# Gathers held to their turns, scatters moved behind a branch, and one set of codes a turn later, in an attention and mixture-of-experts kernel

## The chip, the cores and the metric

The kernel runs on one core of a Trainium2 chip. The metric is the device time of one execution in microseconds (us); the time given for the kernel before is the median of three runs. PE is the matrix engine (TensorE), PEld its weight loads, DVE is VectorE, ACT is ScalarE, POOL is GpSimd, and SP is the engine that here only issues loads and stores.

## The reference

Two blocks stand one behind the other. The first is attention among clusters: query and key attend to each other only where both have the same nearest centroid. The second is a mixture of experts with one expert per token, chosen by cosine similarity.

```python
# B, H, S, D = 4, 8, 768, 64; 16 clusters for each head
q_assign = argmax(einsum('bhsd,hcd->bhsc', q_n, c_n), -1)   # q_n, c_n: normalized
k_assign = argmax(einsum('bhsd,hcd->bhsc', k_n, c_n), -1)
scores = q @ k.T / sqrt(D), with -1e9 where q_assign != k_assign
attn_out = softmax(scores) @ v                              # (B, H, S, D)

x = attn_out.transpose(0, 2, 1, 3).reshape(3072, 512)       # tokens
logits = (xn @ en.T) / tau                                  # 8 experts, unit rows
e = argmax(logits, 1);  gate = softmax(logits)[e]
out = gate * (relu(x @ w1[e]) @ w2[e])                      # w1: 512x1024, w2: 1024x512
```

All inputs and outputs are in float32.

## The kernel before, in words

**Attention.** The 32 heads are worked as 16 pairs `n` of two heads each (`n = 4*b + nb`). A pair has 12 units, two halves of the queries times six blocks of 128 keys. For each unit `scores(m)` has PE multiply queries and keys, with a second, low-precision product with one-hot cluster codes (`hot`) that pushes pairs of different clusters down; `expo(m)` is ACT's exp into a buffer `prob`; `attend(m)` is PE's product with the values. A bank of scores is written again only when its exp has read it; there are two. The loop goes over turns of two units: in turn `it` of pair `n`, with `i = 2*(6*n + it)`, it emits scores and exp of units `i+2` and `i+3`, then work for other stages, and then `attend` of units `i` and `i+1`.

The one-hot codes of the next pair are made in pieces that ride along: `turn0`, `turn1` and `choose` find the nearest centroid on DVE, and `codes` has ACT write the codes (L501, L504) into `cd`, which SP then transposes into `hot` by a DMA (L508). Pair `n+1` reads `hot` from the first scores of its first unit on, which are emitted in turn 4 of pair `n`.

**Between the blocks.** Finished heads are divided by their sums (`total`, L643 and L652; `divide`, L679), written as token rows to `x_rows` in DRAM by SP (L703), and routed: `products` (L722), `logits`, `norms`, `choose`, all in pieces, batch by batch. The places of the tokens of the first three batches are known before the last batch is done (`pa`); those of the last come later (`pb`).

**Experts.** Tokens are gathered by expert. There are 20 items: four "early" ones `E0[0..3]` with 128 tokens each out of the first three batches, and then 16 `later` ones of two kinds, "block" (128 tokens) and "sized" (one for each expert, 160 to 272 tokens in the rows shown by the profile). An item needs its gathers (POOL, `fetches`, four indirect DMAs for an early item, L1144), their transposition (`turn_x`, DVE L1262), weights `w1s` and `w2s` (SP, 2 MB each, L1194), `hidden` (PE L1386, Relu on ACT L1393; for sized items L1293 and L1300), `result` (PE L1426, gating on ACT L1437, L1340 and L1355 on DVE for sized ones) and its scatters to the output (POOL, L1155).

The order of the work on each engine is the order in which the code emits it, set by hand for PE, DVE, ACT, POOL and SP; an instruction that waits holds up all that stand behind it on its engine. Gathers of the early items are emitted by `early_lot(j, n, behind)`: the next `n` gathers of `E0[j]`, and, where `behind` is given, first a one-element POOL copy of that tile, so that the gathers can't start before it is written. In the attention these calls hang on a turn `(b, nb, it)` in the table `early`. Gathers and scatters of the later items lie in a list `queue` with a due item each; `pump(n, behind)` emits `n` of them, and `share(i, left, behind)` emits a share of those that are due at item `i`, where `left` tells how many more such places there are.

Item 13 of 15 (`i == LAST - 2`), a block, has between its two halves of `result` the region `overflow()`: a branch (L1732) for more tokens than expected, which isn't taken with this input. All engines pass through the branch. On its empty side POOL waits for its DMAs that are still out.

Of the kernel before, what the change touches and what calls it, by code (L numbers as in the profile page):

```python
# [9 lines left out]
F32 = mybir.dt.float32  # L10
# [29 lines left out]
def kernel(  # L40
# [12 lines left out]
    nc = tc.nc  # L53
# [4 lines left out]
    F = moe_w1.shape[2]  # L58
    N = B * S
    NJ = S // P  # L60
    NHP = H // 2
# [1079 lines left out]
    mo = {}  # L1141
# [104 lines left out]
    def turn_x(it, evict=None, xT=None):  # L1246
        d = mo[it]
        if it.kind == "sized":
            n = WIDE[it.j]
            d["xT"] = szp.tile([P, KD, SQ * max(WIDE)], F32, tag="xTs", name="xTs")  # L1250
            for u in range(0, n, NQ):
                m = min(NQ, n - u)
                nc.vector.transpose(
                    d["xT"][:, :, SQ * u : SQ * u + SQ * m].rearrange(
                        "p c (w t) -> p w c t", t=SQ
                    ),
                    d["xs"][:, u : u + m].rearrange("p w (c i) -> p w c i", i=SQ),
                )
            return
        d["xT"] = mop.tile([P, DM], F32, tag="xTm", name="xTm") if xT is None else xT  # L1260
        if it.kind == "block" or it in E0[1:]:
            nc.vector.transpose(  # L1262
                d["xT"].rearrange("p (c w t) -> p w c t", c=KD, t=SQ),
                d["xin"].rearrange("p w (c i) -> p w c i", i=SQ),
            )
            return
        bk = psX.tile([P, DM], F32, tag="x_ps", name="x_ps")
        for c in range(KD):
            nc.tensor.transpose(
                bk[:, P * c : P * c + P], d["rows"][:, c].rearrange("p w i -> p (w i)"), ident  # L1270
            )
        evict(d["xT"], bk)
# [99 lines left out]
    def hidden(it, halves=(0, 1)):  # L1372

        d = mo[it]
        for half in halves:
            if half == 0:
                d["hT"] = (
                    flat(szp.tile([P, KF, max(CAPS)], F32, tag="hTs", name="hTs", bufs=1))[:, 0:F]
                    if it.kind == "whole"
                    else mop.tile([P, F], F32, tag="hT", name="hT")  # L1380
                )
            f0 = 512 * half
            bk = psH.tile([P, 512], F32, tag="h_ps", name="h_ps")
            for m in range(0, 512, P):
                for c in range(KD):
                    nc.tensor.matmul(  # L1386
                        bk[:, m : m + P],
                        lhsT=w1s[it.slot][:, c, f0 + m : f0 + m + P],
                        rhs=d["xT"][:, P * c : P * c + P],
                        start=(c == 0),  # L1390
                        stop=(c == KD - 1),
                    )
            nc.scalar.activation(d["hT"][:, f0 : f0 + 512], bk, ACTF.Relu)  # L1393
# [21 lines left out]
    def result(it, halves=(0, 1)):  # L1415
# [44 lines left out]
        (3, 2, 3): lambda: fetch(E0[0]),  # L1460
        (3, 2, 5): lambda: order_x(E0[0]),
        (3, 3, 1): pa.spread_pieces,
        (3, 3, 2): lambda: early_lot(1, 2),
        (3, 3, 3): lambda: early_lot(1, 1),
        (3, 3, 4): lambda: early_lot(1, 1),
        (3, 3, 5): lambda: early_lot(2, 1),
    }
    early_jobs = {}

    def early_lot(j, n, behind=None):  # L1470

        if j not in early_jobs:
            early_jobs[j] = fetches(E0[j])
        if behind is not None:
            nc.gpsimd.tensor_copy(pace, behind)
        for job in early_jobs[j][0:n]:
            job()
        del early_jobs[j][0:n]
# [81 lines left out]
    with tc.manual_schedule(engines=by_hand):  # L1560
        begin()
        for i in range(0, len(units), 2):
            n, it = divmod(i // 2, NJ)

            if n == it == 0:
                load(2, "qk")
            if it == 2 and n + 1 < NP:
                load(n + 1, "v")
            if it >= 4 and n + 3 < NP:
                load(n + 3, "qk"[it - 4])  # L1570
            for m in range(max(i + 2, 6), min(i + 4, len(units))):
                scores(m)
                expo(m)
                if it == 2 and m == i + 2:
                    piece(n + 1, "codes")
            if i == 0:
                begun()
                continue
            between(n, it)
            if it == 4 and n == NP - 1:  # L1580
                divide(2 * n)
            b, nb = divmod(n, NHP)
            if (b, nb, it) in early:
                early[b, nb, it]()
            if it >= 4:
                piece(n + 2, f"turn{it - 4}")
            if i + 2 == len(units):
                ats.close()
                tile_waits = {"side": "right", "reuse_waits": "tile"}
                psX = ctx.enter_context(tc.tile_pool(name="psX", bufs=1, space=PSUM, **tile_waits))  # L1590
                turn_x(E0[0], nc.scalar.copy, xp.tile([P, DM], F32, tag="acc", name="xTm", bufs=3))
            for m in range(max(i, 3), i + 2):
                attend(m)
            if it == 2:
                if n > 0:
                    divide(2 * n - 2, 2 * n - 1)
                unite(2 * n)
            elif it == 5:
                unite(2 * n + 1)
            if i + 2 == len(units):  # L1600
                rows(ngroups - 2)
                route[b][0](0)
            if it == 0 and n > 0:
                total(2 * n - 2, 2 * n - 1)
            if it == 0 and n > 0:
                piece(n + 1, "products")
            if (nb, it) == (0, 4) and b > 0:
                route[b - 1][0](0, 1)
            if it == 3 and n == NP - 1:
                total(2 * n)  # L1610
# [11 lines left out]
        pb = Places(1, rtb)  # L1622
        gates = gate_pieces(0, B - 1)
        gates[0]()
        early_lot(2, 1)
        logits(0)
        hidden(E0[0], (0,))
        turn_x(E0[1])
# [6 lines left out]
        gates[1]()  # L1635
        gates[2]()
        hidden(E0[0], (1,))
        turn_x(E0[2])
        gates[3]()
        early_lot(3, 2, mo[E0[0]]["hT"][0:1, F - 1 : F])  # L1640
        weights1(E0[2])
        read(0, NJ, P - SQ, P)
        products(1)
        hidden(E0[1], (0,))
        logits(1)
        choose()
        early_lot(3, 2, mo[E0[1]]["hT"][0:1, 511:512])
        hidden(E0[1], (1,))
        weights1(E0[3])
        pb.ranks()  # L1650
        pb.firsts()
# [22 lines left out]
        queue = []  # L1674
# [82 lines left out]
        for i, it in enumerate(later):  # L1757
            if i == LAST - 1:
                weights1(later[LAST])
                weights2(later[LAST])  # L1760
            wide = it.kind == "sized"
            if wide:
                order_w2(it)
            if i > 1 and i + 1 < len(later):
                turn_x(later[i + 1])
            made = None
            if i > 0 and later[i - 1].kind == "sized":
                made = mo[later[i - 1]]["ys"][0:1, 0, 0:1]
                queue.extend((min(i + 1, LAST - 2), f) for f in sends(later[i - 1]))
            if 0 < i < LAST - 1 and later[i + 2].kind == "sized":  # L1770
                jobs_of(later[i + 2], i)
            for k in range(i + 2, i + 4):
                if wide and block(k) and later[k] not in mo:
                    jobs_of(later[k], i)
            if wide:
                sized_hidden(it, lambda f, x: share(i, 7 - f // 2, x) if f % 2 else None)
                if i == 1:
                    turn_x(later[2])
                if i + 2 < LAST:
                    weights1(later[i + 2])  # L1780
                    weights2(later[i + 2])
                sized_result(it, lambda g, x: share(i, 3 - g, x) if g < 3 else None)
            elif i < LAST:
                share(i, 3, made)
                hidden(it, (0,))
                share(i, 2, mo[it]["hT"][0:1, 511:512])
                hidden(it, (1,))
                share(i, 1, mo[it]["hT"][0:1, F - 1 : F])
                if i == 0:
                    turn_x(later[1])  # L1790
                    pb.gates(slot_gates)
                if i + 2 < LAST:
                    weights1(later[i + 2])
                result(it, (0,))
                if i == LAST - 2:
                    overflow()
                result(it, (1,))
                if i == 0:
                    jobs_of(later[2], 1)
                    spread_gates()  # L1800
                if i + 2 < LAST:
                    weights2(later[i + 2])
            else:
                pump(len(queue))
                nc.gpsimd.drain()  # L1805
                hidden(it)
                result_last(it)
# [43 lines left out]
```

## Time and profile before

| what | value |
|---|---|
| median of three runs | 698.12 us (696.0 to 698.7) |
| profiled execution, its own time | 695.11 us |
| its span in the trace | 693.0 us |
| PE busy | 682.6 us, 99% |
| DVE, ACT, POOL busy | 382.8, 262.2, 275.6 us |
| DMA queues, share of 16 engines | SP's queue 65.0%, POOL's 5.6% |
| granted TensorE clock | 0.998 |

Times within the profile are counted from the start of the span. The execution that was profiled is 3.0 us below the median, so a difference is worked out against its own time and then laid on the median. A row of the timeline gives the start, the time to the end of the group, engine, line, operation, output and input, and how many instructions; in brackets stands the idle time of the engine before it and what ended it.

### The profile page before, as it was taken

How to read it: one execution, taken by the hardware profiler on the slowest of the kernel's cores; microseconds unless marked ns; L12 is line 12 of the kernel's file. 1: busy time of each engine (PE TensorE's matmuls, PEld its weight loads, DVE VectorE, ACT ScalarE, POOL GpSimd, SP SyncE). 2: the span in 40 equal slices, each digit the busy share in tenths (PEclk: the TensorE clock that was granted, in tenths of full speed). 3: DMA queues.
4: the chain of work that ended last, by engine and by line, in shares of the span. 5: the costliest groups of instructions: out<-in, count | busy, mean ns of one | idle time of the engine just before them, and what ended most of it. 6: DMA issues, size and time to landing. Idle time of an engine off the chain costs nothing. (4 is left out here: it accounts for less than half of the span.)

```text
span 693.0 us, 16339 instructions
## 1 busy us (share of the span) xinstructions
PE 682.6 (99%) x6521; PEld 460.4 (66%) x6521; DVE 382.8 (55%) x673; ACT 262.2 (38%) x444; POOL 275.6 (40%) x505
## 2 busy tenths in 40 slices
PE   8999999999999999999999999999999999999987
PEld 4544444444544444445866678888979797979785
DVE  6898998999899999997674122140301203030310
ACT  6665665576566765574242120101010101111011
POOL 2221222322131222343526343676756465647403
PEclk9999999999999999999999999999999999999999
DMA  9757755776678687689699957457787686878630
GB/s 147 121 82 116 114 100 86 153 141 106 108 131 163 139 147 142 171 209 292 175 311 388 372 189 268 147 175 279 281 282 280 202 301 231 306 249 310 242 133 33
DMA packets 244956, 135.55 MB, mean 196 GB/s; under 512 B 208640, under 2 KB 208642, under 8 KB 244876
## 3 DMA queue, kind: packets, MB, share of 16 engines
q1 hardware_dynamic: 238540, 121.29, 65.0%
q0 software_dynamic: 6160, 13.12, 5.6%
q8 instruction: 53, 0.87, 0.5%
q14 instruction: 27, 0.22, 0.1%
q10 hardware_dynamic: 176, 0.05, 0.0%
HBM read 115.93 MB, written 13.12 MB: 186 GB/s over the span
## 5 line engine op out<-in xcount | busy, mean ns | idle before, releaser
L582 ACT ACTIVATE prob<-s_ps 128x768 f32<-128x768 f32 x192 | 154.0, 814 | 104.7 <-PE s_ps L571 98.6
L571 PE MATMUL s_ps<-qT,kT 64*64 64x384 f32 x1536 | 156.9, 483 | 0.0
L593 PE MATMUL o_ps<-prob,v 64*64 64x385 f32 x1536 | 143.3, 484 | 0.6 <-issue 0.6
L612 DVE TENSOR_TENSOR acc<-acc,prob 128x768 f32<-128x768 f32 x128 | 121.5, 949 | 8.9 <-ACT prob L582 0.5
L593 PEld LDWEIGHTS o_ps<-prob,v 64*64 64x64 f32 x1536 | 58.6, 133 | 66.4 <-issue 58.1
L1340 DVE STREAM_TRANSPOSE ys<-y_ps 128x256 f32<-128x256 f32 (+4 forms) x16 | 6.1, 403 | 154.4 <-PE y_ps L1331 126.6
L1386 PEld LDWEIGHTS h_ps<-xTm,w1s 128*128 128x128 f32 x768 | 87.3, 192 | 2.0 <-issue 1.6
L1386 PE MATMUL h_ps<-xTm,w1s 128*128 128x128 f32 x768 | 88.3, 276 | 0.0
L571 PEld LDWEIGHTS s_ps<-qT,kT 64*64 64x64 f32 x1536 | 55.7, 133 | 35.9 <-issue 31.7
L1426 PE MATMUL y_ps<-w2s,hT 128*128 128x512 f32 x176 | 77.8, 594 | 0.3 <-PEq L1732 0.3
L1293 PE MATMUL h_ps<-xTs,w1s 128*128 128x272 f32 (+7 forms) x384 | 72.9, 346 | 1.8 <-ACT hTs L1300 1.8
L627 POOL COPY behind<-acc 1x1 f32<-1x1 f32 x30 | 6.7, 222 | 168.3 <-DVE acc L612 159.5
L1293 PEld LDWEIGHTS h_ps<-xTs,w1s 128*128 128x128 f32 x384 | 66.7, 190 | 8.6 <-issue 2.9
L1393 ACT ACTIVATE hT<-h_ps 128x512 f32<-128x512 f32 x24 | 14.3, 596 | 147.3 <-PE h_ps L1386 107.8
L1155 POOL DMA_INDIRECT out_dram<-ys,spidx x56 | 55.8, 997 | 33.9 <-issue 19.5
L571 PE MATMUL s_ps<-hot 64*64 64x384 bf16 x768 | 64.6, 325 | 0.1
L1144 POOL DMA_INDIRECT xs<-x_rows,gpidx x56 | 56.8, 1013 | 18.7 <-issue 18.7
L1426 PEld LDWEIGHTS y_ps<-w2s,hT 128*128 128x128 f32 x176 | 32.5, 190 | 37.4 <-issue 36.3
L571 PEld LDWEIGHTS <-hot 64*64 64x64 bf16 x768 | 24.2, 106 | 43.4 <-issue 41.5
L1331 PE MATMUL y_ps<-hTs,w2o 128*128 128x272 f32 (+7 forms) x256 | 48.0, 346 | 0.0
L1331 PE MATMUL misc<-hTs,w2o 128*128 128x272 f32 (+7 forms) x256 | 48.0, 346 | 0.0
L664 POOL COPY inv<-inv 32x12 f32<-32x12 f32 x120 | 31.5, 262 | 36.8 <-DVE inv L661 32.6
(285 smaller groups left out, 740.3 us busy)
## 6 DMA issues: line engine op xcount, KB each, us to landing
w1s<-in_moe_w_dram SPq DMA_DIRECT2D x18, 2048.0 KB
w2s<-in_moe_w_dram SPq DMA_DIRECT2D x18, 2048.0 KB
q<-in_q_dram SPq DMA_DIRECT2D x64, 96.0 KB
k<-in_k_dram SPq DMA_DIRECT2D x64, 96.0 KB
v<-in_v_dram SPq DMA_DIRECT2D x120, 48.0 KB
x_rows<-xb SPq DMA_DIRECT2D x60, 96.0 KB
xr<-x_rows SPq DMA_DIRECT2D x9, 512.0 KB
w1s<-in_moe_w_dram SPq DMA_DIRECT2D x4, 1024.0 KB
```

The lines of the kernel that those rows point to most:

```text
L571: nc.tensor.matmul(s_ps[D * half : D * half + D, h, 0:HS], lhsT=l[rows, half], rhs=r[rows], start=part == (1 if len(parts) < 2 else 0), st ...
L582: nc.scalar.activation(d["prob"][:, :, 0:HS], d["s_ps"][:, :, 0:HS], ACTF.Exp, scale=scale)
L593: nc.tensor.matmul(g["o_ps"][D * h : D * h + D, half, 0:HE], lhsT=ld[n]["v"][keys, j, h], rhs=d["prob"][keys, h, 0:HE], start=(j == 0), st ...
L612: nc.vector.tensor_tensor(g["acc"], g["acc"], d["prob"][:, :, 0:HS], ALU.add)
L664: nc.gpsimd.tensor_copy(inv2[M * to : M * to + M, :, i % 2], inv[M * i : M * i + M])
L1144: nc.gpsimd.indirect_dma_start(out=to, out_offset=None, in_=of, in_offset=bass.IndirectOffsetOnAxis(ap=at, axis=0), bounds_check=n - 1, oo ...
L1155: inst = nc.gpsimd.indirect_dma_start(out=to, out_offset=bass.IndirectOffsetOnAxis(ap=at, axis=0), in_=of, in_offset=None, bounds_check=n - 1,
L1293: nc.tensor.matmul(bk, lhsT=w1s[it.slot][:, c, P * f : P * f + P], rhs=d["xT"][:, c, 0:C], start=(c == 0), stop=(c == KD - 1),)
L1331: nc.tensor.matmul(bks[g][:, 0:C], lhsT=d["w2"][:, f, P * g : P * g + P], rhs=d["hT"][:, f, 0:C], start=(f == 0), stop=(f == KF - 1),)
L1386: nc.tensor.matmul(bk[:, m : m + P], lhsT=w1s[it.slot][:, c, f0 + m : f0 + m + P], rhs=d["xT"][:, P * c : P * c + P], start=(c == 0), stop ...
L1393: nc.scalar.activation(d["hT"][:, f0 : f0 + 512], bk, ACTF.Relu)
L1426: nc.tensor.matmul(bk, lhsT=d["hT"][:, P * c : P * c + P], rhs=w2s[it.slot][:, c], start=(c == 0), stop=(c == KF - 1),)
```

## The change

Three edits. First, the four early gathers of `E0[1]` are emitted one in each of turns 2 to 5 of the last pair, each behind a POOL copy of the `prob` of that turn's first unit (units 184, 186, 188, 190); before, turns 2 to 5 emitted 2, 1, 1 and, of `E0[2]`, 1 with nothing to wait for, and one more of `E0[2]` followed right after the attention. Those two of `E0[2]` now go behind the second half of the hidden stage of `E0[0]`, and the gathers of `E0[3]` move one place on; `turn_x(E0[2])` goes behind `choose`. The copies write a small tile `behind` of their own, since `pace` doesn't exist yet in the attention. Second, of the six scatters of sized item 12, two stay ahead of the branch region in item 13, and four become due at item 14, where `sized_hidden` calls `share` behind every second Relu. Third, in pair 0 the `codes` of the next pair are emitted in turn 3 rather than turn 2; the other pairs keep turn 2.

```diff
-        (3, 3, 2): lambda: early_lot(1, 2),
-        (3, 3, 3): lambda: early_lot(1, 1),
-        (3, 3, 4): lambda: early_lot(1, 1),
-        (3, 3, 5): lambda: early_lot(2, 1),
+        **{(3, 3, it): lambda it=it: early_lot(1, 1, ahead(3, 3, it)) for it in (2, 3, 4, 5)},
     }
+    def ahead(b, nb, it):
+        return un[2 * (NJ * (NHP * b + nb) + it)]["prob"][0:1, 0, 0:1]
...
         if behind is not None:
-            nc.gpsimd.tensor_copy(pace, behind)
+            at = smp.tile([1, 1], F32, tag="behind", name="behind", bufs=1)
+            nc.gpsimd.tensor_copy(at, behind)
...
-                if it == 2 and m == i + 2:
+                if it == (2 if n else 3) and m == i + 2:
                     piece(n + 1, "codes")
...
         gates[0]()
-        early_lot(2, 1)
         logits(0)
         hidden(E0[0], (0,))
         turn_x(E0[1])
...
         hidden(E0[0], (1,))
-        turn_x(E0[2])
         gates[3]()
-        early_lot(3, 2, mo[E0[0]]["hT"][0:1, F - 1 : F])
+        early_lot(2, 2, mo[E0[0]]["hT"][0:1, F - 1 : F])
         weights1(E0[2])
...
         choose()
+        turn_x(E0[2])
         early_lot(3, 2, mo[E0[1]]["hT"][0:1, 511:512])
         hidden(E0[1], (1,))
+        early_lot(3, 2, mo[E0[1]]["hT"][0:1, F - 1 : F])
...
-                queue.extend((min(i + 1, LAST - 2), f) for f in sends(later[i - 1]))
+                due = LAST - 1 if i == LAST - 2 else min(i + 1, LAST - 2)
+                queue.extend((due, f) for f in sends(later[i - 1]))
...
-                share(i, 3, made)
+                if i == LAST - 2:
+                    pump(2, made)
+                else:
+                    share(i, 3, made)
                 hidden(it, (0,))
-                share(i, 2, mo[it]["hT"][0:1, 511:512])
+                if i < LAST - 2:
+                    share(i, 2, mo[it]["hT"][0:1, 511:512])
                 hidden(it, (1,))
-                share(i, 1, mo[it]["hT"][0:1, F - 1 : F])
+                if i < LAST - 2:
+                    share(i, 1, mo[it]["hT"][0:1, F - 1 : F])
```

## The prediction

> **What bounds the kernel now.** I read the page's busy times first, then the timeline at the three places that the diff touches, each for one question: does PE stop there, and for whom?
>
> ```profile
> PE 682.6 (99%) x6521; PEld 460.4 (66%) x6521; DVE 382.8 (55%) x673; ACT 262.2 (38%) x444; POOL 275.6 (40%) x505
> ```
>
> PE is busy for 99% of 693.0 us, so only what stops PE or slows it counts; a freed POOL or DMA second is worth nothing by itself. An edit gains at most what PE loses at its place now.
>
> First place, pair 0 (start, length, then in brackets the idle time before and its releaser):
>
> ```profile
> 20.64 0.41 ACT L501 ACTIVATE cd<-pm,wcd 128x24 bf16<-128x24 bf16 x1 [0.41 <-DVE pm L481]
> 21.51 0.81 ACT L582 ACTIVATE prob<-s_ps 128x768 f32<-128x768 f32 x1
> ...
> 22.37 0.11 PEld L571 LDWEIGHTS <-hot 64*64 64x64 bf16 x3 [0.50 <-issue]
> ...
> 23.14 1.56 SPq L508 DMA_TRANSPOSE hot<-cd  x1
> ...
> 27.25 0.11 PEld L571 LDWEIGHTS <-hot 64*64 64x64 bf16 x4 [0.35 <-DMA hot<-cd]
> ```
>
> The codes wait for DVE and stand ahead of unit 7's exp, whose bank scores(9) needs: PE's hot part starts at 22.37, where its step of 0.81 from 21.27 gives 22.08, a loss of 0.29. The codes' transpose is issued at 23.14 (SP has v loads until 22.97) and PE's weight load at 27.25 waits for it: the matmul at 27.37 is just on PE's pitch of 2.91, so this transfer has no slack at all.
>
> Second place, the end of the attention:
>
> ```profile
> 308.08 1.46 PE L593 MATMUL o_ps<-prob,v 64*64 64x385 f32 x16
> ...
> 312.32 1.03 POOL L1144 DMA_INDIRECT xin<-x_rows,early_i  x1 [0.28 <-POOL inv L664]
> ...
> 318.10 2.31 PE L593 MATMUL o_ps<-prob,v 64*64 64x385 f32 x13
> ...
> 319.19 1.00 POOL L1144 DMA_INDIRECT xin<-x_rows,early_i  x1 [0.30 <-issue]
> ...
> 320.98 0.87 PE L593 MATMUL o_ps<-prob,v 64*64 64x385 f32 x3 [0.57 <-issue]
> ...
> 321.06 1.51 ACT L582 ACTIVATE prob<-s_ps 128x768 f32<-128x768 f32 x2 [3.77 <-remote]
> ```
>
> The sixteen attend matmuls take 1.46 at 308.08 and 3.75 at 318.10 (to 321.85): 2.3 lost. With the wider gaps at 315.29 and 316.09 (0.60 where 0.18 is usual) and the 0.86 that PE then waits for the late exp (322.71), it is about 3.4. Six gathers run from 312.32 to 320.19, their packets move from 316 to 324.
>
> Third place, the region of the overflow branch:
>
> ```profile
> 650.49 0.98 POOL L1155 DMA_INDIRECT out_dram<-ys,spidx  x1 [0.57 <-issue]
> 650.64 0.39 SPq L1194 DMA_DIRECT2D w1s<-in_moe_w_dram  x1
> ...
> 651.77 0.97 POOL L1155 DMA_INDIRECT out_dram<-ys,spidx  x1 [0.30 <-DVE xTm L1262]
> ...
> 659.68 0.69 ACT L1437 ACTIVATE y<-y_ps,slot_gates 128x512 f32<-128x512 f32 x1 [10.07 <-DMA xin<-x_rows,gpidx]
> ...
> 660.61 3.53 PE L1293 MATMUL h_ps<-xTs,w1s 128*128 128x160 f32 x24 [1.77 <-ACT hTs L1300]
> ```
>
> PE's y_ps is ready at 654.49, but y starts at 659.68, and the Relus behind it free PE's banks only then: 1.77 lost. The releaser named, xin, had landed long before. POOL's empty branch waits for all its DMAs still out, and ACT's y behind the region waits for that; by the semaphore records POOL passed at 659.4, after the sixth scatter (issued 651.77) had landed at 657.8.
>
> **What the skill says.** (1) "DMA: Bandwidth & Descriptors", SWDGE vs HWDGE vs iDMA: each DMA engine takes turns between internal queues that software (POOL) and hardware (SP) descriptors feed. The trace agrees: the first scatter of this item lands in 2.7 us (643.36 to 646.1), the sixth in 6.0, among the w1s and w2s packets of 650.64 and 654.52. (2) "Perfetto Trace Analysis", Summary: TensorE's end is an estimate. That fits the stretch at 318: matmuls of unchanged length (0.48 to 0.53 us), while ACT gets its bank at 321.06, long after the modelled end of its scores (318.60). (3) "Runtime: NRT & Kernel Launch", Instruction fetch mechanics: instructions come in blocks of 256 ahead of need. The trace shows PE's blocks fetched at 312.35 and 328.12 and none in the stretch, so that is not its cause.
>
> **Part C, codes one turn later.** Removed: ACT's 0.41 wait and 0.84 of codes between exp 6 and exp 7; PE gets its 0.29 back. Added: the same codes behind exp 8. On ACT that is o_sb at about 21.5 to 22.3, exp 8 to 23.15, codes to 24.0; exp 9 then ends at 24.8, before scores(11) needs its bank at 24.98, so nothing else is late. SP issues the transpose at 24.05 instead of 23.14; SP's q loads behind it (24.82) slip by 0.9, and are wanted a pair later. It took 4.06 us; the other pairs' mostly 3.6 to 4.0. I take 3.9: landed at 27.95, PE's matmul at about 28.1 instead of 27.37: **+0.7**, the earlier 0.29 already used up in it. Bounds: −0.3 (a much quicker transfer), +0.9 (4.06 again).
>
> **Part B, four scatters behind the region.** At item 13 only two scatters stay ahead; they are today's at 643.36 and 644.70, landed by 646.8, before the region (650.5) and the w1s load. POOL passes at about 651 at latest; y starts when y_ps is ready (654.5), the Relus follow: **−1.75** (1.6 to 1.8). The four scatters go behind Relus 1, 3, 5, 7 of item 14: 4 × (1.00 + 0.18 copy + 0.15) = 5.3 us of POOL, which idles 7.90 ahead of 660.64 and from 661.6 to 675.4. Their DMA stands beside w1s and w2s, which keep the engines full until 664.0; w2s is wanted at 673.6, so 9 us cover them, and with that cover gone each costs PE what it delays the load, about 1. The last item's own scatters start at 675.4 as now. No new wait there: y's scatter is issued before them, and later scatters wait for nothing of theirs.
>
> **Part A, gathers held.** Removed from 317.89 and 319.19: E2's two gathers, to 336.4 and 337.8, the old places of E3's; E3's four go to 340.9, 342.2 and about 344.2, 345.5; the four gate gathers slip by 2 × 1.3 + copy and wait, about 3.3, to 346.9 to 352. E1's four stay: POOL's inv copies end at 312.05, after exps 184 and 186, so the first three hardly move (about 312.5, 314.2, 316.1); the fourth waits for exp 190, 318.6 to 322.7. E3's land by about 352 and are wanted by turn_x(E0[3]) at 360.57. Four copies of 0.18 on idle POOL cost nothing; exp 190, which writes the buffer of prob 184 again, must wait for the first copy, done by 312.5, 6 us earlier. The gate's y (350.26) slips to about 353.5, POOL's scatter and rr22b (L1024) behind it end by 357.9; PE's tokens (L1040) want it at 359.12: 1.2 of cover, beyond which PE pays 1:1. turn_x(E0[2]) behind choose on DVE fits ahead of L873 (342.27; landed 340.3). E1's turn_x (327.17) waits for the fourth gather: in front of DVE's L652 (330.20) it has until about 329.5.
>
> What the stretch at 316 to 322 owes to gathers is not shown. Bounds: nothing, and the 3.4. For them speaks that it starts and ends with their packets, and that two 1 MB loads with no gathers at 304 to 308 left PE's pitch alone. Against: the MoE half has gathers beside loads with no such gaps, and three of the six stay. I take **−3.0**: the exp 188 to 190 region would have one gather instead of three.
>
> Sum: 0.7 − 1.75 − 3.0 = **−4.05**, on the profiled execution's own 695.11 (span 693.0 and 2.1 around it) 691.1. The median of the runs shown is 698.12, 3.0 higher; the same step from there gives **694.1**.
>
> **The rivals.** P, the stretch stays: its cause is w1s and w2s (1 MB at 311.22, 2 MB at 311.81) with the x_rows stores (four, in small packets, issued 315.50 to 323.3), all of which stay. For it: the DMA engines are full from 312 to 324. Against: the 304 to 308 loads. Sum −1.05, 697.1; half-way 695.6. S, slower: the fourth gather of E1, held behind an exp 190 that is itself late (322.7), lands late; DVE stands in turn_x(E0[1]) and behind it L652 (2.56) and L679 (0.62), for which PE's products(1) at 333.85 waits. It decides the sign from a landing at about 331, a latency over 8.3; the longest seen is 6.6. At 10 us (332.7) PE loses 2.8: −1.05 + 2.8 = +1.8, **699.9**; at 12 us +3.8, 701.9. Speaking for it: DMA is full there. Against: the last x_rows stores end by 324. That the change doesn't do what it says: holding moves three of E1's gathers by nothing; this is inside P.
>
> **How the numbers follow.** The runs differ by 2.7 and a measurement here can tell about 0.5%, 3.5 us: faster means under 694.6, slower over 701.6. Main case 0.53, of which 0.06 falls short of −3.5; P with its half-way 0.31, all within; S 0.16, of which 0.10 is over +3.5 with a C at its upper bound or a cover of the gate's chain gone as well, 0.06 within. So faster 0.47, same 0.43, slower 0.10. The range: from the main case at its best (−3.4 − 1.8 − 0.3 = −5.5, 692.6) to S's 699.9; some 0.1 lies above it and a little below.
>
> **What the profile after would show.** C: codes at about 23.1, transpose at 24.05, PE's load waiting near 28.0. B: y near 654.5, with no 1.77 in front of the third group of hidden matmuls, four scatters between 655 and 665. A: E1's gathers at 312.5 to 322.7; right if the attends near 318 take about 1.5, P if they still take over 3. S if DVE's turn_x(E0[1]) waits past 330 for xin. I am wrong in size if the transpose lands before 27, or if PE stops at L1040 for rr22b.

## The result and the profile after

The changed kernel took 690.41 us (median of six runs, 690.06 to 690.56), the kernel before beside it 698.49 (six runs, 696.0 to 699.32): a ratio of 0.9888, 95% interval 0.9873 to 0.9903. That is 8.1 us less, where 4.0 were forecast, and lies under the low end of the range (692.6). The profiled execution took 690.41 as well, its span is 688.2 us; against the profiled execution of before (695.11, span 693.0) the step is 4.7 to 4.8 only.

The busy times of the changed kernel's page:

```profile
PE 680.6 (99%) x6521; PEld 459.1 (67%) x6521; DVE 383.6 (56%) x673; ACT 262.8 (38%) x444; POOL 276.7 (40%) x512
```

PE is still busy for 99%. Its own timeline at the first place, pair 0:

```profile
23.16 0.39 ACT L501 ACTIVATE cd<-pm,wcd 128x24 bf16<-128x24 bf16 x1
...
24.06 1.56 SPq L508 DMA_TRANSPOSE hot<-cd  x1
...
28.03 0.11 PEld L571 LDWEIGHTS <-hot 64*64 64x64 bf16 x4 [1.30 <-DMA hot<-cd]
```

Codes, transpose and PE's wait stand where they were forecast (23.1, 24.05, 28.0). PE is 0.66 later behind this wait than in the profile before; 0.13 of that it was late from its first matmuls on, so the edit costs about 0.5 here. At the end of the attention:

```profile
313.11 1.04 POOL L1144 DMA_INDIRECT xin<-x_rows,early_i  x1 [0.15 <-POOL behind L1478]
...
314.58 1.46 PE L593 MATMUL o_ps<-prob,v 64*64 64x385 f32 x16
...
318.41 1.46 PE L593 MATMUL o_ps<-prob,v 64*64 64x385 f32 x16
...
319.56 1.02 POOL L1144 DMA_INDIRECT xin<-x_rows,early_i  x1 [0.54 <-issue]
...
321.85 0.87 PE L722 MATMUL misc<-xT,embT 128*32 128x96 f32 x32
```

The attends at 318 take 1.46 again where they took 3.75, and the fourth gather is issued at 319.56, right behind an exp in good time. From the third last attends (314.58) to L722, the first product of the routing (321.85), it is 7.27 us. In the kernel before it was 10.82, so 3.55 are gained:

```profile
313.90 1.46 PE L593 MATMUL o_ps<-prob,v 64*64 64x385 f32 x16
...
324.72 0.87 PE L722 MATMUL misc<-xT,embT 128*32 128x96 f32 x32
```

At the branch:

```profile
642.20 1.00 POOL L1155 DMA_INDIRECT out_dram<-ys,spidx  x1 [0.30 <-issue]
...
651.91 0.69 ACT L1437 ACTIVATE y<-y_ps,slot_gates 128x512 f32<-128x512 f32 x1 [6.86 <-PE y_ps L1426]
...
655.22 0.98 POOL L1155 DMA_INDIRECT out_dram<-ys,spidx  x1 [0.58 <-issue]
...
656.01 3.42 PE L1293 MATMUL h_ps<-xTs,w1s 128*128 128x160 f32 x24
```

The last scatter ahead of the region is issued at 642.20, y waits for PE's y_ps and nothing else, the third group of hidden matmuls starts without the 1.77 of idle time. From the second half of `result` to this group PE takes 7.86 us, 9.79 before. So each step of the sum is there in the trace: about +0.5, −3.55 and −1.9 where +0.7, −3.0 and −1.75 were forecast. Two things were not explained: why the medians differ by 8.1 and not by 4.8, and what the slow stretch near 318 is.

### The profile page after: what moved, and what is told of

Its sections match the earlier page's. It is cut to its first block, busy times and chain, and to the rows that moved or that the text cites. A ratio compares the mean times of both kernels' runs of the same rounds, so it can differ in the third digit from the quotient of the medians.

```text
span 688.2 us, 16351 instructions
## 1 busy us (share of the span) xinstructions
PE 680.6 (99%) x6521; PEld 459.1 (67%) x6521; DVE 383.6 (56%) x673; ACT 262.8 (38%) x444; POOL 276.7 (40%) x512
## 5 line engine op out<-in xcount | busy, mean ns | idle before, releaser
L593 PE MATMUL o_ps<-prob,v 64*64 64x385 f32 x1536 | 141.5, 484 | 0.0
```

Source lines behind the costliest of these rows:

```text
L593: nc.tensor.matmul(g["o_ps"][D * h : D * h + D, half, 0:HE], lhsT=ld[n]["v"][keys, j, h], rhs=d["prob"][keys, h, 0:HE], start=(j == 0), st ...
```

## The experiments

### Each edit by itself

Three kernels have one edit of the change each (the hunks are those of the diff above), one has the gathers' and the scatters' edits together:

```diff
# a_only: table `early`, ahead(), early_lot(), the moved early_lot() calls, turn_x(E0[2])
# b_only: due, pump(2, made), no share() at item 13
# c_only
-                if it == 2 and m == i + 2:
+                if it == (2 if n else 3) and m == i + 2:
# ab: a_only and b_only
```

> The kernel before with only the gathers' edit (E1's four held to turns, E2's two and E3's moved, turn_x(E0[2]) behind choose). The profiles gave the whole change 4.8 us between two single executions, the medians 8.1. Theory 1 (the rest of the gain, about 3 us, is in the slow stretch, which in most executions of the kernel before is longer than the 3.4 us of the profiled one): this edit alone gives -6 to -7, about 691.8, and its runs agree within 0.6 us. Theory 2 (the gathers give 3.4 in every execution; the rest is elsewhere, in the region's wait): -3.4, about 695, and the runs are spread over 2 us or more as those of before.

> The kernel before with only the four scatters of item 12 behind the region. Theory 1: -1.8 to -2.1, about 696.5, with runs spread as those of before. Theory 2 (the wait in the region is longer in most executions than in the profiled one): -5, about 693.5, and the spread gone.

> The kernel before with only the codes of pair 1 made one turn later. Theory 1 and 2: the transfer into hot lands 0.7 us past PE's pitch and nothing gives it back: +0.5 to +0.8, about 699.1. A third: the later codes shift the end of the attention against the loads and so change the slow stretch, then a difference of more than 2 us either way is to be seen.

> The changed kernel with the codes of pair 1 back in turn 2, so the gathers' and the scatters' edits alone. If the codes' edit costs what the profile shows: 0.7 below the changed kernel, 689.7, with runs within 0.6 us. If its 0.7 is hidden by later waits: 690.4 as the changed kernel.

They ran on chip 3. The kernel before took **690.0** there (49 runs), not 698.5. Beside it: gathers alone 689.86, ratio 1.0001 (0.9992 to 1.0009); scatters alone 690.13, 1.0002 (0.9993 to 1.0010); codes alone 690.52, 1.0007 (0.9999 to 1.0015); gathers and scatters 689.85, 0.9998 (0.9990 to 1.0007). Both theories missed: nothing was to be gained here, since the kernel before had lost nothing. The codes' cost of 0.5 is the only edit whose mean moves, and its interval still takes in no change.

### Both kernels again

No edit.

> The kernel before, unchanged, for its profile beside the others: with each edit alone the kernel took 689.9 to 690.5, and the kernel before, run beside them, 690.0, while the first comparison had it at 698.5. Theory 1 (the slow stretch at the end of the attention and the late Relu ahead of the branch are not in the kernel's schedule; they are disturbances that the first executions had and these have not): span 687.4 to 688.7, attend matmuls near 318 in 1.46, y at the branch within 1.5 us of its y_ps, with the six gathers at the same places. Theory 2 (they are in it, and something else is faster by as much): the attends near 318 take over 3 us again.

> The changed kernel, unchanged, beside the kernel before. Theory 1: within 0.6 us of 690.4 as in the first comparison, so +0.4 against the kernel before: the codes' 0.7 less what is won at the branch. Theory 2 (the gain of 8.1 holds wherever the two are run side by side): 1.1% below the kernel before.

On chip 14: the kernel before 689.84, the same program beside it 689.75 (0.9998, 0.9990 to 1.0007); the changed kernel 690.11, ratio 1.0004 (0.9995 to 1.0013). Theory 1 holds: what the change removed in the first comparison isn't there. (One of its details missed: y is 2.0 behind its y_ps, where 1.5 at most were expected.) The timeline of the kernel before on this chip, at the second and third place:

```profile
317.81 1.46 PE L593 MATMUL o_ps<-prob,v 64*64 64x385 f32 x16
...
319.28 1.10 POOL L1144 DMA_INDIRECT xin<-x_rows,early_i  x1 [0.30 <-issue]
...
647.09 0.97 POOL L1155 DMA_INDIRECT out_dram<-ys,spidx  x1 [0.30 <-POOLq L1732]
647.59 0.39 SPq L1194 DMA_DIRECT2D w1s<-in_moe_w_dram  x1
...
653.43 0.69 ACT L1437 ACTIVATE y<-y_ps,slot_gates 128x512 f32<-128x512 f32 x1 [8.76 <-DMA xin<-x_rows,gpidx]
...
655.62 3.42 PE L1293 MATMUL h_ps<-xTs,w1s 128*128 128x160 f32 x24
```

The six gathers stand within 0.1 us of their times in the first profile, and PE keeps its pace of 1.46 beside them. At the branch the sixth scatter leaves 0.5 us ahead of the w1s load; y still waits for it (653.43, 2.0 behind its y_ps), but PE never stops. In the trace of the changed kernel PE is 0.89 later at 28.4, but 0.46 of that stands there from 7 us on, ahead of anything that the edits touch: executions differ so much in their start. The run of the gathers' and scatters' edits on this chip (the last section of experiments) starts as late as the changed kernel and lacks only the codes' edit. Between these two traces the codes' edit costs PE 0.56 at 28.8 and 0.49 at its end.

### A late Relu, put in by hand

In the first profile the second Relu of item 13 started 1.9 us behind its matmuls, whose end in the trace is 647.08:

```profile
649.01 0.60 ACT L1393 ACTIVATE hT<-h_ps 128x512 f32<-128x512 f32 x1 [4.87 <-remote]
```

Doing it four times over puts POOL's copy and the last two scatters behind it late in the same way:

```diff
# relu_late (n = 4), relu_one (n = 2); relu_late_scat: n = 4 and the scatters' edit
+            for _ in range(n if it is later[-3] and half else 1):
                 nc.scalar.activation(d["hT"][:, f0 : f0 + 512], bk, ACTF.Relu)
# dense: eight gathers in turns 2 to 5
-        (3, 3, 3): lambda: early_lot(1, 1),
-        (3, 3, 4): lambda: early_lot(1, 1),
-        (3, 3, 5): lambda: early_lot(2, 1),
+        (3, 3, 3): lambda: early_lot(1, 2),
+        (3, 3, 4): lambda: early_lot(2, 2),
+        (3, 3, 5): lambda: early_lot(2, 2),
...
-        early_lot(2, 1)
-        early_lot(2, 2, mo[E0[0]]["hT"][0:1, 511:512])
```

> The kernel before with the second Relu of item 13 done four times over (same values), so that POOL's copy behind it and the last two scatters of item 12 come 1.8 us later, as they did in the first profile, where that Relu started 1.9 us after its matmuls (649.01, 647.08). Theory 1 (the loss at the branch was the schedule's answer to that late Relu: scatters five and six fall behind the w1s and w2s loads, POOL's wait in the region holds ACT's y): the sixth scatter lands about 4 us later than in the kernel before, y about 5 us after y_ps, PE idle 1.5 to 2.5 us ahead of the third group of sized hidden matmuls; 691.5 to 692.5. Theory 2 (the branch's loss needs more than that, some disturbance of the chip): under 690.3.

> The same late Relu, with the four scatters of item 12 moved behind the region (the scatters' edit alone). Theory 1: nothing waits for scatters in the region, the loss is gone: 690.0 to 690.3. If the loss comes from the longer ACT work and not from the scatters: as with the late Relu alone.

> The kernel before with eight gathers, rather than six, one after the other at the end of the attention (E1's four and E2's four in turns 2 to 5, none behind them), so that they run from about 312 to 322.5 without a stop. Theory 1 (gathers do not slow PE): attends near 318 in 1.46, 690.0 within 0.6. Theory 2 (PE lost 3.4 us to gathers): some gaps of 0.5 us between groups of four matmuls near 317 to 322 and 691 to 694.

On chip 9, the kernel before at 689.9: the late Relu 692.09, ratio 1.0037 (1.0023 to 1.0051); with the scatters moved 690.05, 1.0001 (0.9992 to 1.0010); eight gathers 689.83, 0.9998 (0.9989 to 1.0006). The timeline with the late Relu:

```profile
648.32 0.97 POOL L1155 DMA_INDIRECT out_dram<-ys,spidx  x1 [0.30 <-DVE xTm L1262]
...
656.31 0.69 ACT L1438 ACTIVATE y<-y_ps,slot_gates 128x512 f32<-128x512 f32 x1 [10.15 <-DMA xin<-x_rows,gpidx]
...
657.24 3.53 PE L1293 MATMUL h_ps<-xTs,w1s 128*128 128x160 f32 x24 [1.85 <-ACT hTs L1300]
```

and with the scatters' edit beside it:

```profile
651.63 0.69 ACT L1438 ACTIVATE y<-y_ps,slot_gates 128x512 f32<-128x512 f32 x1 [4.97 <-PE y_ps L1427]
...
655.73 3.42 PE L1293 MATMUL h_ps<-xTs,w1s 128*128 128x160 f32 x24
```

The first is the picture of the profile before, in nearly its numbers: sixth scatter behind the w1s load, y 5.26 behind its y_ps, PE idle for 1.85 (5.19 and 1.77 there). The second has the same late Relu and no loss. So it is shown that late scatters delay the region, the region y, and y PE, and that the scatters' edit cuts this chain. The eight gathers left PE's attends at 1.46: here gathers alone don't slow PE.

### How near the edge the kernel before stands

> The kernel before with the second Relu of item 13 done twice, so 0.6 us later. Two traces agree on one sum: PE loses what y is late behind its y_ps, plus 0.93, minus 4.35 (5.19 gave 1.77, 5.26 gave 1.85). Theory 1 (a threshold): the sixth scatter is issued at about the time of the w1s load, y is 2 to 3 us late, under the 3.42 that cost nothing: 690.0 within 0.3. Rival (the loss grows with the delay): a third of the 2.2 that the thrice repeated Relu cost, 690.6.

> The gathers' edit alone once more, in case this chip is one on which the kernel before takes 696 to 699. There: if that edit takes the slow stretch away, 3.5 to 6 us below the kernel before; if not, under 2. On a chip on which the kernel before takes 690: the same 689.9 as before.

> The scatters' edit alone once more, for the same reason. On a chip on which the kernel before takes 696 to 699: 1.8 to 2.1 below it if the stretch is the gathers' affair. On a chip on which it takes 690: 690.1.

On chip 14 again, the kernel before at 690.08: the Relu done twice 691.16, ratio 1.0010 (1.0001 to 1.0019); gathers alone 689.91, 0.9993 (0.9985 to 1.0000); scatters alone 690.25, 0.9996 (0.9985 to 1.0006). Timeline with the Relu done twice:

```profile
647.46 0.97 POOL L1155 DMA_INDIRECT out_dram<-ys,spidx  x1 [0.30 <-issue]
647.59 0.39 SPq L1194 DMA_DIRECT2D w1s<-in_moe_w_dram  x1
...
655.77 0.69 ACT L1438 ACTIVATE y<-y_ps,slot_gates 128x512 f32<-128x512 f32 x1 [10.47 <-DMA xin<-x_rows,gpidx]
...
656.70 3.53 PE L1293 MATMUL h_ps<-xTs,w1s 128*128 128x160 f32 x24 [0.91 <-ACT hTs L1300]
```

The expected 690.0 was wrong, its formula right: y is 4.33 late, and 4.33 + 0.93 − 4.35 = 0.91 is what PE loses. I had taken the scatter's delay for that of y. (4.35 − 0.93 = 3.42 us is what y can be late at no cost to PE.) The sixth scatter is issued only 0.37 us later than in the kernel before (647.46, 647.09), but its landing is signalled at 653.88 rather than 651.54, and POOL passes the region 1.7 us after that. Between these two traces each tenth of a microsecond nearer to w1s cost six tenths, and the kernel before stood 1.4 us of y ahead of the edge (2.0 late, 3.42 free).

### A chip on which the kernel before is slow

```diff
# a_third is a_only, b_third is b_only; a_moved_only: E1's gathers as before, E2's and E3's moved
-        (3, 3, 5): lambda: early_lot(2, 1),
...                                           # and the later early_lot() calls as in the change
```

> The gathers' edit alone. Where the kernel before takes 696 to 699 as in the first comparison: 3.5 to 6 us below it if holding and moving the gathers is what takes the slow stretch away. Where it takes 690: 689.9.

> The scatters' edit alone. Where the kernel before takes 696 to 699: 1.8 to 2.1 below it. Where it takes 690: 690.1.

> Half of the gathers' edit: E2's and E3's gathers moved as in the change, E1's four not held. Where the kernel before takes 696 to 699: as the whole edit if the number of gathers matters, as the kernel before if their turns do. Where it takes 690: 689.9, since no gather is seen to cost PE anything there.

These three ran on chip 7, and the kernel before took **696.05** there (10 runs, 695.34 to 698.06). Gathers alone 692.91, ratio 0.9964 (0.9945 to 0.9983); scatters alone 693.50, 0.9963 (0.9950 to 0.9975); E2's and E3's gathers moved without holding E1's 693.14, 0.9956 (0.9940 to 0.9973). Neither edit's gain is of the size expected: 3.1 us in the medians where 3.5 to 6 were, and 2.6 where 1.8 to 2.1 were. The timeline with the gathers' edit alone:

```profile
318.04 1.46 PE L593 MATMUL o_ps<-prob,v 64*64 64x385 f32 x16
...
644.78 1.10 POOL L1155 DMA_INDIRECT out_dram<-ys,spidx  x1 [0.30 <-issue]
646.68 0.60 ACT L1393 ACTIVATE hT<-h_ps 128x512 f32<-128x512 f32 x1 [5.32 <-remote]
...
658.41 3.53 PE L1293 MATMUL h_ps<-xTs,w1s 128*128 128x160 f32 x24 [2.36 <-ACT hTs L1300]
```

with the scatters' edit alone:

```profile
318.65 0.90 PE L593 MATMUL o_ps<-prob,v 64*64 64x385 f32 x3
...
321.19 0.90 PE L593 MATMUL o_ps<-prob,v 64*64 64x385 f32 x6 [0.54 <-issue]
...
647.53 0.60 ACT L1393 ACTIVATE hT<-h_ps 128x512 f32<-128x512 f32 x1 [2.98 <-PE h_ps L1386]
...
659.08 3.15 PE L1293 MATMUL h_ps<-xTs,w1s 128*128 128x160 f32 x22
```

and with E2's and E3's gathers moved only:

```profile
318.79 1.76 PE L593 MATMUL o_ps<-prob,v 64*64 64x385 f32 x13
...
647.87 0.60 ACT L1393 ACTIVATE hT<-h_ps 128x512 f32<-128x512 f32 x1 [5.25 <-remote]
```

Each edit takes away its own loss and leaves the other's. Between the third last attends and L722, where 7.27 is undisturbed, it is 7.26 with the gathers' edit, 10.96 with the scatters' edit only, and 8.41 when E2's gathers are merely moved: of 3.7 us, moving away two gathers takes 2.55 and spreading the other four the rest (in one trace each; the medians don't separate these two). At the branch PE stands 2.36 with the six scatters in place, and not at all with four of them moved. And the late Relu itself (ends of the matmuls 644.30 and 645.56, Relu 2.4 and 2.3 us later) is gone with the scatters' edit: 647.53, at once behind PE.

That points to a common cause, which can be counted. For each half of a hidden stage of an early or block item I counted POOL's gathers and scatters issued in the 4 us ahead of its last matmul's modelled end, and took the time from that end to its Relu (without one half near 331, where ACT loads a table first, 1.07 in every trace). "Late" is over 0.35 us.

| POOL's indirect DMAs in the 4 us | first comparison and chip 7 (5 traces): late, mean delay | chips 3, 9, 14 (9 traces): late, mean delay |
|---|---|---|
| 0 or 1 | 0 of 19, 0.05 us | 0 of 46, 0.05 us |
| 2 | 6 of 44, 0.21 us | 0 of 99, 0.04 us |
| 3 | 37 of 52, 1.06 us | 0 of 62, 0.05 us |

In the first five traces the Relu came 0.4 to 2.6 us late in 37 of 52 halves with three such DMAs ahead; in the nine others, and in the three of the next section, it never did. It is PE's signal that is late: in the profile before, the semaphore that this Relu of item 13 waits for is updated at 648.99, 1.9 behind the modelled end, and ACT starts 0.02 after it. Whether the matmuls themselves end late, modelled ends can't tell.

A count alone could stand for something else in these places, and 15 of the 52 were in time. But where an edit moves the DMAs, the delay moves with them, both ways. The second half of item 13 has two ahead of it with the scatters' edit, and its Relu comes in 0.04 us. The first half of E0[2] has one ahead of it in the kernel before and with the scatters' edit (Relu after 0.1), and three once E3's gathers are moved: on chip 7 and in the first comparison its Relu is then 1.45 to 1.81 late, on chip 14 with the same three DMAs 0.1. Whether their issue or their packets do it isn't separated.

The stretch at 318 lies beside six gathers in a row. That it has the same cause is argued from this and from the three edits above, not shown: there PE issues its matmuls late, beside the Relus it doesn't. Whether it belongs to the chip or to what else ran there at the time the record doesn't show either: chip 14 was met three times and was always undisturbed, chip 7 once.

### Twice the dose, and the other half

```diff
# held_only: the holding alone, E2's two gathers still at the end of the attention
+        **{(3, 3, it): lambda it=it: early_lot(1, 1, ahead(3, 3, it)) for it in (2, 3, 4)},
+        (3, 3, 5): lambda: (early_lot(1, 1, ahead(3, 3, 5)), early_lot(2, 1)),
# dense_again is dense, ab_again is ab
```

> The other half of the gathers' edit: E1's four gathers each behind the prob of their turn, with the two of E2 still following them at the end of the attention. On a chip on which the kernel before takes 696: if spreading E1's gathers is what matters, PE keeps its pace at 318 and the kernel is about 3 us below the one before; if the number of gathers matters, PE loses over 2 us there as before. On a chip on which it takes 690: 690.0.

> Eight gathers in a row instead of six, again. On a chip on which the kernel before takes 696: if the gathers are what slows PE, 1 us or more above the kernel before, with slow groups of attends until about 324; if not, as the kernel before. Where it takes 690: 689.8 as the first time.

> The gathers' and the scatters' edits without that of the codes. On a chip on which the kernel before takes 696: their single gains of 3.1 and 2.6 add up, and it is 0.4 below the changed kernel, about 690.0. Where it takes 690: 689.85 as before.

They met chip 14, with the kernel before at 690.04, and tell nothing of the other condition: 689.94, ratio 0.9997 (0.9989 to 1.0006), 689.95, 0.9996 (0.9988 to 1.0005), and 689.86, 0.9999 (0.9990 to 1.0007). They repeat that on such a chip held, dense and moved gathers are all one. Whether eight gathers cost more than six where six cost 3.7 was therefore not seen.

## Why the prediction was right and wrong

**Codes.** Right in mechanism, with the transpose at 24.06 and PE at 28.03. As a term of the sum +0.7 was a little too high: it cost 0.56 at its place and 0.49 at PE's end between two traces that start alike, and 0.5 in the medians of chip 3.

**Scatters.** Right in mechanism and nearly in size: −1.75 was forecast; PE's wait was 1.77 and 2.36 in two traces that have it, and the edit alone gave 2.6 on chip 7. What I called the kernel's schedule was only half of it: the six scatters reach past the w1s load only if the Relu ahead of the last two is late, as the run with the late Relu shows; with that Relu on time the kernel before loses nothing there. That on such a chip the Relu is late because of the scatters themselves, as the edits on chip 7 indicate, was not seen at all.

**Gathers.** −3.0 was taken between 0 and 3.4; the trace gave −3.55, and −3.1 in the medians of chip 7. What the coincidence with their packets spoke for held on such a chip; on the three others the same six gathers slow nothing. That the 3.4 came near was luck in part: the gaps of 0.60 at 315.29 and 316.09 that it counts as loss stand in the undisturbed trace of chip 14 too (315.38 and 316.17). The rest of the loss lay just behind them: the attends at 318 start 4.20 us behind those before them, 3.83 on chip 14. The argument against the gathers, that the experts' part has some beside loads "with no such gaps", looked at PE alone: the signs were there as late Relus (behind matmuls that end at 371.4, 464.5, 539.1 and 681.1 in the profile before), for which PE didn't have to stop. The 0.4 that the −3.0 left for the gathers that stay was not needed: spread over 6.5 us they cost none.

**The step that failed** is the one from the sum to the median: "the median of the runs shown is 3.0 higher; the same step from there". It carried −4.05 over unchanged, and so gave the change no share in the 3.0 that a median run takes beyond the profiled one, without a reason. The profiled execution was a run of before with a small loss; I laid the gain on the median as if the other 3.0 were the kernel's own time. They weren't: between the profiles the step is 4.7, between the medians 8.1. The kernel before takes 689.8 on chip 14, so it lost 8.6 in the first comparison; the changed kernel, at 690.4 there and 690.1 on chip 14, lost 0.3. That the changed kernel merely ran on a better chip is not borne out: the record doesn't name the chip, but the changed kernel's trace there has late Relus too (up to 2.6 us), as only the traces of this comparison and of chip 7 have. The spread of the runs of before (already 2.7 in the three shown then; 0.5 for the changed kernel) was the sign for it, and I used it only to widen what can be told apart. In what place the runs at 698 lost their last 3 us no trace shows, and so not by which edit they were won; that stays open. One trait is on record: the six runs of the experiments with a granted clock of 0.996, where all others have 0.998 to 1.000, were 1.0 to 4.2 us over their kernel's median, among them the two longest of the kernel before on chip 7 (697.63 and 698.06). In the first comparison the clock of the runs of before isn't on record; the six of the changed kernel had 0.999 to 1.000. A lower clock may thus be part of those 3 us, and of the gain of 8.1; whether it is cause or consequence isn't shown.

**Rivals.** P fell: w1s, w2s and x_rows stay where they were within 0.7 us, and the stretch went. S didn't come: xin landed in time, turn_x(E0[1]) ran at 325.26. The remark that instruction blocks aren't the cause stands, and on better ground than it had: in the two traces with the whole stretch PE's block is fetched at 312.35 and 312.31, but at 312.62 with the late Relu and at 312.65 with the scatters' edit on chip 14, where the attends take 1.46. What a chip has or lacks that it answers to POOL's DMAs in this way is open. The Trainium skill's remark that a DMA engine takes turns between the queues of software and hardware descriptors ("DMA: Bandwidth & Descriptors", SWDGE vs HWDGE vs iDMA) fits what was seen at the branch: a scatter issued 0.37 us later landed 2.34 us later once the w1s packets were beside it.

## What to carry to other kernels

Where the runs of a kernel spread by 3 us and its profile is one of the short ones, ask what that spread is made of before laying a gain on the median: a change that takes away its cause can gain the spread too. And run both versions on more than one chip: this one is worth 1.1% on one, some 0.7% on a second if the gains of its two parts add up, and nothing, whole or in parts, on three. Here gathers and scatters that are spread over the work, each behind a piece of it, cost nothing where they were harmless (ratio 0.9998) and guarded the kernel where they weren't.

## What the hardware showed that I had not expected

The same program took 690 us on three chips, and 696 and 698 in two other measurements, with a granted clock of 0.998 to 1.000 in the traces of both kinds. In the latter PE's signals came up to 2.6 us late, mostly where POOL had issued three gathers or scatters 1.3 us apart just before, and in one place PE issued groups of four matmuls every 0.72 us instead of 0.32 for 4 us; the durations of the single matmuls in the trace don't change.
